# Gathering expert rows two experts ahead in a routed two-layer MLP behind attention

## The chip, the cores and the metric

One core of a Trainium2 chip runs the whole program in one launch. The metric is the device time of that launch in microseconds (us), the median over several runs. TensorE is PE in the profile (PEld is its weight load), VectorE DVE, ScalarE ACT, GpSimd POOL and SyncE SP.

## What is computed

Attention with normalised queries and keys (8 batches, 12 heads, 448 tokens, head size 64) gives 3584 token rows of 768 values. A hash of each token's id then picks one of 8 experts, and the row goes through that expert's two layers:

```python
expert_idx = token_ids * np.int64(2654435761) % np.int64(E)
for e in range(E):
    mask = expert_idx == e
    h = np.maximum(x[mask] @ w1[e], 0.0)    # w1[e]: 768 x 1024
    out[mask] = h @ w2[e]                   # w2[e]: 1024 x 768
```

## The kernel before, in words

The first stage, attention, writes its rows as 16-bit values to a scratch tensor in device memory (`x_scratch`), batch by batch, and builds a table `gidx` with the row numbers of each expert: four tiles of 128 rows (KT = 4, CAP = 512) for each of the 8 experts. A tile's first three quarters hold rows of the first seven batches only, so three of an expert's four tiles can be fetched before the last batch is stored; the fourth tile needs all batches.

The second stage, the experts, is what the change touches. For each expert `e` the loop at line 840 does this:

- `fetch` (lines 781 to 785) gathers tiles of 128 rows x 768 values (197 KB) from `x_scratch` into row buffers `xg`, one indirect DMA each, issued by POOL (line 173). The pool `m_xg` has 8 such buffers, zeroed once on DVE at lines 830 to 832.
- `gemm1` (line 747) multiplies w1 by the transposed rows `xT`: 48 matmuls, with ACT and DVE writing the result through a maximum with zero into `h_sb`.
- For each of the four tiles, `turn` (line 787) transposes one gathered tile of the *next* expert (six 128x128 transposes on PE at line 184 into the only buffer of `ps_x`, one DVE copy at line 185), and `gemm2` (line 761) makes one output tile of this expert: 16 matmuls (line 765), a copy to one of five `o_sb` buffers (line 769, ACT and DVE in turn), and an indirect DMA that scatters the 128 rows of 768 32-bit values (393 KB) to the output (line 770, POOL).
- `w_next` (line 813) issues weight pieces, also by POOL (line 816). An expert's weights come in six pieces that are converted from 32 to 16 bit on the way: four of 393 KB (w1) and two of 786 KB (w2). During expert `e` the six pieces of expert `e + 3` go out: two behind the gathers at its start, and one behind each of its four scatters. Two weight buffers each in `w_pool` and `w_pool2` hold four experts.

So POOL issues everything that moves in this stage, in program order: gathers, weight pieces, scatters. In the kernel before, expert `e + 1` is gathered at the start of expert `e` (line 848) and turned between the outputs of expert `e`.

Expert 0 differs. Its first three tiles are fetched and turned inside attention. Ahead of the loop (lines 833 to 838) the order is: three tiles of expert 1, one piece of expert 2's weights, the last tile of expert 0, the last tile of expert 1, the other five pieces of expert 2. In the loop, expert 0 first does `gemm1` for its first 384 rows and three outputs with no turns between them; then (lines 853 to 857) it turns its own last tile and all four tiles of expert 1 in a row, does `gemm1` for its last 128 rows, and the fourth output.

Of the kernel before, what the change touches and what calls it, by code (L numbers as in the profile page):

```python
# [19 lines left out]
def kernel(  # L20
# [16 lines left out]
    E = moe_w1.shape[0]  # L37
# [12 lines left out]
    KT = CAP // P  # L50
# [121 lines left out]
    def gather(xg, idx, rows=N):  # L172
        nc.gpsimd.indirect_dma_start(  # L173
            out=xg[:], out_offset=None, in_=x_dram[0:rows, :],
            in_offset=bass.IndirectOffsetOnAxis(ap=idx, axis=0),
            bounds_check=rows - 1, oob_is_err=False)
        return xg
# [3 lines left out]
    def put_xT(xg, xT, col, bank, copy=None):  # L181
        xT_ps = bank.rearrange("p (c t) -> p c t", c=CO)
        for co in range(CO):
            nc.tensor.transpose(xT_ps[:, co, :], xg[:, co * P:(co + 1) * P], ident16[:])  # L184
        (copy or nc.vector.tensor_copy)(xT[:, :, col * P:(col + 1) * P], xT_ps)  # L185
# [13 lines left out]
    with tc.manual_schedule(), \  # L199
# [461 lines left out]
        for g in range(1, NG):  # L661
            t = s0[g - 1]
# [69 lines left out]

    with tc.manual_schedule(), \
         tc.tile_pool(name="w_pool2", bufs=2) as w_pool2, \
         tc.tile_pool(name="m_xg", bufs=8) as m_xg, \
         tc.tile_pool(name="m_rt", bufs=1) as m_rt, \
         tc.tile_pool(name="m_x", bufs=2) as m_x, \
         tc.tile_pool(name="m_h", bufs=2) as m_h, \
# [8 lines left out]
        def gemm1(w1_sb, xT, h_sb, c0, c1):  # L747
            w1v = w1_sb[:].rearrange("p c (f o) -> p c o f", o=FO)
            for fo in range(FO):
                h_ps = ps_h.tile([P, 512], FP32, name="h_ps")  # L750
                for co in range(CO):
                    nc.tensor.matmul(h_ps[:, :c1 - c0], lhsT=w1v[:, co, fo, :],  # L752
                                     rhs=xT[:, co, c0:c1],
                                     start=(co == 0), stop=(co == CO - 1))
                if fo % 2 == 0:
                    nc.scalar.activation(h_sb[:, fo, c0:c1], h_ps[:, :c1 - c0], AF.Relu)  # L756
                else:
                    nc.vector.tensor_scalar(out=h_sb[:, fo, c0:c1], in0=h_ps[:, :c1 - c0],  # L758
                                            scalar1=0.0, scalar2=None, op0=ALU.max)

        def gemm2(w2_sb, h_sb, col, idx, free=True):
            o_ps = ps_o.tile([P, DIN], FP32, name="o_ps")
            for d0, d1 in ((0, 512), (512, DIN)):
                for fo in range(FO):
                    nc.tensor.matmul(o_ps[:, d0:d1], lhsT=h_sb[:, fo, col * P:(col + 1) * P],  # L765
                                     rhs=w2_sb[:, fo, d0:d1],
                                     start=(fo == 0), stop=(fo == FO - 1))
            o_sb = m_o.tile([P, DIN], FP32, name="o_sb")
            (nc.vector.tensor_copy if col % 2 else nc.scalar.copy)(o_sb[:], o_ps[:])  # L769
            scat = nc.gpsimd.indirect_dma_start(  # L770
                out=out[:, :], out_offset=bass.IndirectOffsetOnAxis(ap=idx, axis=0),
                in_=o_sb[:], in_offset=None, bounds_check=N - 1, oob_is_err=False)
            if free:

                tc.declare_no_dep(scat.ins, group="scatters", reason="disjoint rows")
                tc.add_to_no_dep_group("scatters", scat.ins)
# [4 lines left out]
        def fetch(e, kts):  # L781
            for kt in kts:
                c = e * KT + kt
                xgs[c] = gather(m_xg.tile([P, DIN], FP16, name="xg"), gidx[:, c:c + 1],
                                N_EARLY if kt < KT - 1 else N)

        def turn(e, kt):
            if e not in xTs:
                xTs[e] = m_x.tile([P, CO, CAP], FP16, name="xT")
            bank = ps_x.tile([P, DIN], FP16, name="xT_ps")  # L790
            put_xT(xgs.pop(e * KT + kt), xTs[e], kt, bank[:])

        def w_pieces(e):

            pool = wp(e)
            w1_sb = pool.tile([P, CO, F], FP16, name="w1_sb")
            w2_sb = pool.tile([P, FO, DIN], FP16, name="w2_sb")
            w_tiles[e] = (w1_sb, w2_sb)
            src1 = moe_w1[e].rearrange("(j ph hh pl) f -> ph pl hh j f", ph=2, hh=2, pl=64)
            src2 = moe_w2[e].rearrange("(p fo) d -> p fo d", fo=FO)  # L800
            dst1 = [w1_sb[64 * ph:64 * ph + 64].rearrange("p (hh j) f -> p hh j f", hh=2)
                    for ph in range(2)]
            res = []
            for ph in range(2):
                for hh in range(2):
                    res.append((dst1[ph][:, hh], src1[ph][:, hh]))
            for q4 in range(0, FO, 4):
                res.append((w2_sb[:, q4:q4 + 4], src2[:, q4:q4 + 4]))
            return res
# [3 lines left out]
        def w_next(n):  # L813
            for _ in range(min(n, len(queue))):
                o, i = queue.pop(0)
                nc.gpsimd.dma_start(out=o, in_=i)
# [5 lines left out]
        def overflow_table():  # L822
            nc.vector.tensor_tensor(out=ovc[:],
                                    in0=iota_f[:, 0:NOV, None].to_broadcast([P, NOV, E]),
                                    in1=oend[:, None, :].to_broadcast([P, NOV, E]), op=ALU.is_ge)
            nc.vector.reduce_sum(ovf[:], ovc[:], axis=AX.X)
            nc.vector.tensor_scalar(out=ov_i[:], in0=ovf[:], scalar1=float(E - 1), scalar2=None,
                                    op0=ALU.min)

        for t in range(8):  # L830
            z = m_xg.tile([P, DIN], FP16, name="xg")
            nc.vector.memset(z[:], 0.0)
        fetch(1, range(KT - 1))
# [1 line left out]
        w_next(1)  # L835
        fetch(0, [KT - 1])
        fetch(1, [KT - 1])
        w_next(len(queue))
        queue += w_pieces(3)
        for e in range(E):  # L840
            w1_sb, w2_sb = w_tiles[e]
            h_sb = m_h.tile([P, FO, CAP], FP16, name="h_sb")
            if e == 0:
                gemm1(w1_sb, xTs[e], h_sb, 0, EARLY)
                overflow_table()
            else:
                if e + 1 < E:
                    fetch(e + 1, range(KT))
                gemm1(w1_sb, xTs.pop(e), h_sb, 0, CAP)
            w_next(2)  # L850
            for kt in range(KT):
                c = e * KT + kt
                if e == 0 and kt == KT - 1:
                    turn(0, kt)
                    for k in range(KT):
                        turn(1, k)
                    gemm1(w1_sb, xTs.pop(0), h_sb, EARLY, CAP)
                elif e > 0 and e + 1 < E:
                    turn(e + 1, kt)
                gemm2(w2_sb, h_sb, kt, gidx[:, c:c + 1])  # L860
                w_next(1)
            w_next(len(queue))
            if e + 4 < E:
                queue += w_pieces(e + 4)
# [47 lines left out]
```

## Time and profile before

| | us |
|---|---|
| median of 3 timed runs (lowest to highest) | 421.67 (420.98 to 424.35) |
| the profiled execution's own time | 423.57 |
| its span, first to last instruction | 422.0 |
| PE busy in the span | 359.6 (85%) |
| DVE, ACT, POOL busy | 215.5, 187.4, 174.7 |

The profile's times are positions in the span, from its first instruction. The 1.57 us between the span and the execution's own time lie outside what the profile shows. Attention ends at about 191 us of the span, and the experts fill the rest. Numbers such as `x48` are counts of instructions; what stands in brackets behind a row of the timeline is the idle time of that engine ahead of it and what ended it.

### The profile page before, as it was taken

How to read it: one execution, taken by the hardware profiler on the slowest of the kernel's cores; microseconds unless marked ns; L12 is line 12 of the kernel's file. 1: busy time of each engine (PE TensorE's matmuls, PEld its weight loads, DVE VectorE, ACT ScalarE, POOL GpSimd, SP SyncE). 2: the span in 40 equal slices, each digit the busy share in tenths (PEclk: the TensorE clock that was granted, in tenths of full speed). 3: DMA queues.
4: the chain of work that ended last, by engine and by line, in shares of the span. 5: the costliest groups of instructions: out<-in, count | busy, mean ns of one | idle time of the engine just before them, and what ended most of it. 6: DMA issues, size and time to landing. Idle time of an engine off the chain costs nothing. (4 is left out here: it accounts for less than half of the span.)

```text
span 422.0 us, 9529 instructions
## 1 busy us (share of the span) xinstructions
PE 359.6 (85%) x4006; PEld 244.4 (58%) x4006; DVE 215.5 (51%) x517; ACT 187.4 (44%) x299; POOL 174.7 (41%) x247
## 2 busy tenths in 40 slices
PE   7776989899999999989898697895995987999970
PEld 3454767667676677657575364563563653666640
DVE  5665989989999999863232122221221321322210
ACT  3754989989999998961111011011110120121110
POOL 9897360046299200152716065262371450423030
PEclk9988999999999999989979699898898996999995
DMA  9999999829999960263999989899599691322020
GB/s 125 165 128 194 182 220 186 146 61 179 188 228 232 232 146 4 67 149 81 187 215 264 182 162 237 138 196 235 103 212 190 142 242 49 127 71 106 20 117 18
DMA packets 54268, 64.60 MB, mean 153 GB/s; under 512 B 22403, under 2 KB 42134, under 8 KB 53968
## 3 DMA queue, kind: packets, MB, share of 16 engines
q0 software_dynamic: 50592, 57.98, 79.0%
q1 hardware_dynamic: 3024, 5.41, 4.7%
q8 instruction: 32, 0.52, 0.5%
q10 hardware_dynamic: 608, 0.59, 0.5%
q14 instruction: 12, 0.10, 0.1%
HBM read 89.68 MB, written 18.09 MB: 255 GB/s over the span
## 5 line engine op out<-in xcount | busy, mean ns | idle before, releaser
L498 ACT ACTIVATE expT<-sc_ps 128x896 bf16<-128x896 f32 x144 | 123.9, 934 | 21.4 <-PE sc_ps L496 21.1
L765 PE MATMUL o_ps<-w_sb,h_sb 128*128 128x256 f16 (+1 forms) x512 | 96.8, 348 | 0.0
L770 POOL DMA_INDIRECT out_dram<-o_sb,gidx x32 | 33.0, 1032 | 118.1 <-ACT o_sb L769 82.9
L765 PEld LDWEIGHTS <-h_sb 128*128 128x128 f16 x512 | 52.0, 104 | 39.1 <-issue 10.0
L752 PEld LDWEIGHTS <-w_sb 128*128 128x128 f16 x432 | 59.8, 146 | 25.3 <-issue 0.8
L752 PE MATMUL h_ps<-xT,w_sb 128*128 128x512 f16 x336 | 73.7, 379 | 0.0
L769 ACT COPY o_sb<-o_ps 128x768 f32<-128x768 f32 x16 | 12.8, 799 | 102.7 <-PE o_ps L765 102.7
L756 ACT ACTIVATE h_sb<-h_ps 128x512 f16<-128x512 f32 (+2 forms) x36 | 19.7, 549 | 85.6 <-PE h_ps L752 85.6
L173 POOL DMA_INDIRECT xg<-x_scratch,gidx x32 | 32.6, 1019 | 59.1 <-DVE x_sb L536 38.3
L758 DVE TENSOR_SCALAR h_sb<-h_ps 128x512 f16<-128x512 f32 (+2 forms) x36 | 22.8, 632 | 59.5 <-PE h_ps L752 59.5
L520 PEld LDWEIGHTS <-expT 128*128 128x128 bf16 x1152 | 43.2, 98 | 9.8 <-issue 5.6
L496 PE MATMUL sc_ps<-qT,kT 64*128 64x448 f16 x288 | 43.5, 358 | 4.4 <-DVE et L385 1.4
L185 DVE COPY xT<-xT_ps 128x768 f16<-128x768 f16 x28 | 15.5, 555 | 61.2 <-PE xT_ps L184 61.2
L520 PE MATMUL av_ps<-v,expT 128*128 128x65 bf16 x1152 | 44.7, 195 | 0.0
L184 PE MATMUL xT_ps<-ident,xg 128*128 128x128 f16 x174 | 16.7, 241 | 26.4 <-DMA xg<-x_scratch,gidx 23.8
L769 DVE COPY o_sb<-o_ps 128x768 f32<-128x768 f32 x16 | 15.3, 958 | 39.8 <-PE o_ps L765 35.5
L475 PE MATMUL qkT_ps<-ident,n 128*128 128x128 f16 x384 | 30.6, 222 | 5.7 <-DVE n L320 3.6
L475 PEld LDWEIGHTS <-n 128*128 128x128 f16 x384 | 22.3, 98 | 20.0 <-issue 12.2
L184 PEld LDWEIGHTS <-xg 128*128 128x128 f16 x192 | 14.6, 108 | 32.0 <-DMA xg<-x_scratch,gidx 26.1
L536 DVE TENSOR_TENSOR x_sb<-av_ps,srec 128x448 f16<-128x448 f32 x48 | 29.7, 619 | 1.5
L287 PEld LDWEIGHTS <-ident 128*128 128x128 f16 x544 | 24.3, 99 | 7.7 <-issue 5.7
L503 ACT ACTIVATE expT<-sc_ps 128x448 bf16<-128x448 f32 x48 | 27.8, 578 | 1.6 <-PE sc_ps L501 1.6
(140 smaller groups left out, 403.2 us busy)
## 6 DMA issues: line engine op xcount, KB each, us to landing
w_sb<-in_moe_w_dram POOLq DMA_DIRECT2D x32, 384.0 KB, 12.0
w_sb<-in_moe_w_dram POOLq DMA_DIRECT2D x12, 768.0 KB, 11.6
x_scratch<-x_sb SPq DMA_DIRECT2D x15, 288.0 KB, 6.0
w_sb<-in_moe_w_dram POOLq DMA_DIRECT2D x2, 1536.0 KB, 16.8
kr<-in_k_dram POOLq DMA_DIRECT2D x6, 384.0 KB, 10.6
qr<-in_q_dram POOLq DMA_DIRECT2D x3, 768.0 KB, 14.8
vr<-in_v_dram POOLq DMA_DIRECT2D x6, 384.0 KB, 19.0
kr<-in_k_dram POOLq DMA_DIRECT2D x6, 288.0 KB, 9.6
```

The costliest lines, as they stand in the source:

```text
L173: nc.gpsimd.indirect_dma_start(out=xg[:], out_offset=None, in_=x_dram[0:rows, :], in_offset=bass.IndirectOffsetOnAxis(ap=idx, axis=0), bou ...
L184: nc.tensor.transpose(xT_ps[:, co, :], xg[:, co * P:(co + 1) * P], ident16[:])
L475: nc.tensor.transpose(T[:, o:o + P], n8[:, a, i, j].rearrange("p h d -> p (h d)"), ident16[:])
L496: nc.tensor.matmul(sc[:, hh, :S], lhsT=kT[64 * hh:64 * hh + 64, P * j:P * j + P], rhs=qT[64 * hh:64 * hh + 64, :], start=True, stop=True)
L498: nc.scalar.activation(expT[:, 2 * j:2 * j + 2, :], sc[:, :, :S], AF.Exp, bias=0.0, scale=1.0)
L503: nc.scalar.activation(expT[:, 6, :], sc[:, 0, :S], AF.Exp, bias=0.0, scale=1.0)
L520: nc.tensor.matmul(av[:, 2 * t + hh, :], lhsT=expT[:, tl(hh, j), P * t:P * t + P], rhs=v8[:, i, 4 * hh + j, 0:D + 1], start=(j == 0), stop ...
L536: nc.vector.tensor_tensor(out=x_sb[:, :, hp * D:hp * D + D], in0=av[:, :, :D], in1=srec[:, :, None].to_broadcast([P, SL, D]), op=ALU.mult)
L752: nc.tensor.matmul(h_ps[:, :c1 - c0], lhsT=w1v[:, co, fo, :], rhs=xT[:, co, c0:c1], start=(co == 0), stop=(co == CO - 1))
L765: nc.tensor.matmul(o_ps[:, d0:d1], lhsT=h_sb[:, fo, col * P:(col + 1) * P], rhs=w2_sb[:, fo, d0:d1], start=(fo == 0), stop=(fo == FO - 1))
L769: (nc.vector.tensor_copy if col % 2 else nc.scalar.copy)(o_sb[:], o_ps[:])
L770: scat = nc.gpsimd.indirect_dma_start(out=out[:, :], out_offset=bass.IndirectOffsetOnAxis(ap=idx, axis=0), in_=o_sb[:], in_offset=None, bo ...
```

## The change

Three edits. The row buffers become ten, and ten are zeroed. Expert `e + 2` is gathered at the start of expert `e` instead of expert `e + 1`, and to start with, all four tiles of expert 2 are gathered ahead of the loop, behind the last tile of expert 1 and in front of the five pieces of expert 2's weights. And expert 1's tiles are turned one ahead of each output of expert 0, as for the other experts, the last of them behind the second `gemm1` of expert 0.

```diff
-         tc.tile_pool(name="m_xg", bufs=8) as m_xg, \
+         tc.tile_pool(name="m_xg", bufs=10) as m_xg, \
...
-        for t in range(8):
+        for t in range(10):
             z = m_xg.tile([P, DIN], FP16, name="xg")
             nc.vector.memset(z[:], 0.0)
         fetch(1, range(KT - 1))
...
         w_next(1)
         fetch(0, [KT - 1])
         fetch(1, [KT - 1])
+        fetch(2, range(KT))
         w_next(len(queue))
...
             else:
-                if e + 1 < E:
-                    fetch(e + 1, range(KT))
+                if e + 2 < E:
+                    fetch(e + 2, range(KT))
                 gemm1(w1_sb, xTs.pop(e), h_sb, 0, CAP)
             w_next(2)
             for kt in range(KT):
                 c = e * KT + kt
                 if e == 0 and kt == KT - 1:
                     turn(0, kt)
-                    for k in range(KT):
-                        turn(1, k)
                     gemm1(w1_sb, xTs.pop(0), h_sb, EARLY, CAP)
-                elif e > 0 and e + 1 < E:
+                    turn(1, kt)
+                elif e + 1 < E:
                     turn(e + 1, kt)
                 gemm2(w2_sb, h_sb, kt, gidx[:, c:c + 1])
                 w_next(1)
```

## Rows read from the trace of the kernel before

**Rows 1.** The page's 40 equal slices of the span: granted clock and DMA share, in tenths.
```profile
PEclk9988999999999999989979699898898996999995
DMA  9999999829999960263999989899599691322020
```

**Rows 2.** Waits of PE from 185 us on: us in total, times, longest.
```profile
PE xT_ps L184 <- DMA xg<-x_scratch,gidx: 23.8, 5, 6.0
```

**Rows 3.** Windows, one per expert 1 to 6: busy and count by engine, clock, DMA share, GB/s.
```profile
219.67:250.12 30.45, 24.44 (x139) 15.20 (x138) 6.82 (x10) 3.98 (x6) 12.14 (x14) 0.89 0.96 215
250.12:278.13 28.01, 23.73 (x138) 14.94 (x137) 6.82 (x10) 3.98 (x6) 12.14 (x15) 0.94 0.92 186
278.13:307.80 29.67, 24.76 (x139) 15.37 (x138) 6.82 (x10) 3.98 (x6) 12.16 (x15) 0.88 0.84 176
307.80:335.99 28.19, 23.90 (x139) 15.02 (x137) 6.82 (x10) 3.98 (x6) 12.17 (x15) 0.94 0.90 184
335.99:365.45 29.46, 25.10 (x138) 15.56 (x137) 6.82 (x10) 3.99 (x6) 8.69 (x10) 0.88 0.53 138
365.45:387.55 22.10, 22.10 (x138) 14.46 (x137) 6.73 (x10) 3.99 (x6) 8.05 (x8) 1.00 0.28 95
```

**Rows 4.** Timeline of PE, first tile of gemm2 for experts 1 and 6.
```profile
236.21 0.82 PE L184 MATMUL xT_ps<-ident,xg 128*128 128x128 f16 x6 [6.01 <-DMA xg<-x_scratch,gidx]
236.82 4.65 PE L765 MATMUL o_ps<-w_sb,h_sb 128*128 128x512 f16 x16
241.31 0.50 PE L184 MATMUL xT_ps<-ident,xg 128*128 128x128 f16 x6
...
375.81 0.50 PE L184 MATMUL xT_ps<-ident,xg 128*128 128x128 f16 x6
...
378.75 0.50 PE L184 MATMUL xT_ps<-ident,xg 128*128 128x128 f16 x6
```

**Rows 5.** Timeline of PE, late attention and expert 0.
```profile
177.70 0.62 PE L475 MATMUL qkT_ps<-ident,n 128*128 128x128 f16 x8
...
195.00 4.06 PE L752 MATMUL h_ps<-xT_e,w_sb 128*128 128x384 f16 x24 [0.65 <-DVE h_sb L758]
198.90 7.96 PE L765 MATMUL o_ps<-w_sb,h_sb 128*128 128x512 f16 x48
206.70 0.50 PE L184 MATMUL xT_ps<-ident,xg 128*128 128x128 f16 x6
207.85 0.49 PE L184 MATMUL xT_ps<-ident,xg 128*128 128x128 f16 x6 [0.65 <-DVE xT_e L185]
...
210.14 0.80 PE L184 MATMUL xT_ps<-ident,xg 128*128 128x128 f16 x6 [0.65 <-DVE xT L185]
...
212.18 5.06 PE L752 MATMUL h_ps<-xT_e,w_sb 128*128 128x128 f16 x48
```

**Rows 6.** Timeline of POOL, ahead of and in the first two experts.
```profile
197.78 1.05 POOL L173 DMA_INDIRECT xg<-x_scratch,gidx  x1 [11.36 <-DVE h_sb L758]
...
200.14 4.31 POOL L816 DMA_DIRECT2D w_sb<-in_moe_w_dram  x7
204.75 1.08 POOL L770 DMA_INDIRECT out_dram<-o_sb,gidx  x1 [0.30 <-issue]
...
231.44 0.65 POOL L816 DMA_DIRECT2D w_sb<-in_moe_w_dram  x1 [2.39 <-DMA w_sb<-in_moe_w_dram]
```

**Rows 7.** Windows: the long queue of experts 0 and 1, and the gap behind it.
```profile
204.00:234.00 30.00, 23.60 (x161) 17.24 (x158) 8.64 (x15) 4.29 (x9) 12.56 (x15) 0.88 1.07 232
...
242.00:244.00 2.00, 2.00 (x14) 1.16 (x12) 0.40 (x1) 0.31 (x1) 1.40 (x2) 1.00 0.03 4
```

**Rows 8.** DMA issues at 197.7 to 198.5 us, then 222 to 228: count, us to landing.
```profile
xg<-x_scratch,gidx POOLq DMA_INDIRECT x1, 3.0
...
xg<-x_scratch,gidx POOLq DMA_INDIRECT x4, 12.9
```

**Rows 9.** Timeline of DVE, the last of the eight buffer clears.
```profile
183.58 0.38 DVE L832 MEMSET xg<- 128x384 uint32 x1
```

## The prediction

> **What bounds the kernel now.** I read the 40 slices of the page first, then the waits of PE, then windows cut at the start of each expert's `gemm1`, then the timelines of PE and POOL inside one expert. In the slices the clock dips again and again in the second half of the span, where the experts run, while DMA stays near full until about 350 us and is little used from there on [rows 1]. The waits say why PE stops there: 23.8 us in five waits of a transpose for gathered rows [rows 2]. That is one wait for each of the experts 1 to 5. Expert 6 has the same work with its rows there in time, and takes 22.10 us at full clock, PE busy throughout; experts 1 to 5 take 30.45, 28.01, 29.67, 28.19 and 29.46 [rows 3]. The reader should see in the PE timeline what such a wait costs twice over: at expert 1 it lasts 6.01 us, and the first transposes and output behind it take 241.31 - 236.21 = 5.10 us where expert 6 needs 378.75 - 375.81 = 2.93 [rows 4]. The clock granted in these experts averages 0.88 to 0.94 against 1.00 [rows 3]: after the idle stretch PE runs for a while at 1.2 GHz and not 2.4. So the stage is bound by PE plus a wait for rows on each expert, and the wait comes from order, not from a slow gather: alone a gather lands 3.0 us after issue, behind weight pieces 12.9 us [rows 8].
>
> **Experts 1 to 5.** With rows gathered one expert earlier, a tile is issued some 22.1 + 10.5 us before its turn, where now it has only the `gemm1` of one expert. If the rows come in time each expert takes expert 6's 22.10. The sum of the five steps is 145.8, less 5 x 22.1 = 110.5: **-35.3 us** [rows 3]. Of it 23.8 is the wait itself [rows 2], the rest clock. Nothing is added to PE or DVE in these steps: the same turns stand at the same places. On POOL the same four gathers stand at the same place, only for another expert; from expert 6 on none are left.
>
> **Expert 0.** Now three outputs without turns take 206.70 - 198.90 = 7.80, or 2.60 each; then come five turns 1.15 apart (206.70 to 207.85), each waiting 0.65 for DVE to empty the one transpose buffer; the fourth turn already runs at half rate (0.80 for what took 0.50), and so does the small `gemm1` behind them, 48 matmuls in 5.06 [rows 5]. `gemm1` of expert 1 starts at 219.67 [rows 3], 20.77 after 198.90. Afterwards: three outputs with a turn each, 3 x 2.93 = 8.8 (expert 1's first three tiles were gathered inside attention and wait already); one turn and its gap, 1.15; the small `gemm1`; a turn, 0.34; an output, 2.60. One gap of 0.65 did not cost the clock at 195.00, where 24 matmuls of 384 columns took 4.06 [rows 5], so I expect the small `gemm1` at 2.4 GHz. Its bounds are 4.9 (as now) and half of that, 2.45; eight transposes of as many columns took 0.62 [rows 5], 78 ns each at most, or 3.7 for 48, last one's drain included each time. I take 2.9, nearer the half. Sum 15.8, so expert 1 starts at 214.7: **-5.0 us** (bounds -5.4 and -3.0).
>
> **Two more clears.** 2 x 0.38 on DVE [rows 9], in the last attention steps. Bounds 0 and +0.8; DVE has idle room behind 184 us, so **+0.2**.
>
> **The moved gathers on POOL.** Four gathers, about 1.3 each with their gap, stand ahead of seven weight pieces that now start at 200.14 and of the first scatter at 204.75 [rows 6]. Pieces and scatters of expert 0 go out some 5.2 late, and POOL has caught up by the fourth scatter (four pairs of scatter and piece, 1.8 each, against outputs 2.93 apart). Behind them wait expert 2's weights, which land by about 220 and are needed at 236.8, and five output buffers, of which expert 0 fills four. **0 us**. If that cover were gone it would cost the 5.2. A further buffer conflict I rule out by order: with ten buffers the four new rows go where rows of an expert already turned lay.
>
> **What is late next: DMA.** This is the only large unknown. Per expert that carries weights the queue moves 4 x 0.393 + 2 x 0.786 (weights) + 4 x 0.393 (scatters) + 4 x 0.197 (gathers) = 5.5 MB. With a long queue, 204 to 234 us, it wrote 232 GB/s [rows 7], which gives 23.7 us per expert. At expert 2 the step of 28.01 had a DMA share of 0.92 [rows 3], 25.8 us of work; the queue ran dry inside that step as it did at 242 us [rows 7], and started again one scatter at a time. Either is above PE's 22.1, so DMA falls behind by 1.6 to 3.7 us per expert, against a cushion. The cushion: expert 2's first tile landed at 236.21 [rows 4] through a queue that stayed full from 202; the same queue with four more gathers (0.79 MB, 3.4 us) lands expert 3's at 239.6, and they are needed at 214.7 + 22.1 + 10.5 = 247.3. That leaves 7.7 us, and four more experts (gathers for 4 to 7) eat at it. With DMA time d per expert, the stall at the end is 4 x (d - 22.1) - 7.7: none at 23.7, 1.9 at 24.5, 7.1 at 25.8. In the new order the queue is always long, so I stand nearer the first row: d = 24.4, **+1.5 us**, at experts 5 and 6. Output buffers have nearly the same cushion (the third scatter of an expert lands about half of d behind the gathers ahead of it and is needed 11.7 us behind them), so they wait with the gathers and not on top. Weights have more: expert 7's are through just ahead of its gathers, about 337 to 343, and needed at 347. POOL already waits at times for an earlier transfer before it issues (2.39 at 231.44 [rows 6]); it will do that more, which moves no landing while the queue is full.
>
> The Trainium skill ("HBM Reference", Specifications) gives a core about 358 GB/s as its share of device memory, and about 425 streaming alone. Counted at that memory a weight byte written is two bytes read, so an expert costs 6.3 + 1.6 + 0.8 = 8.7 MB, an estimate of 24.2 us at the share and 20.4 alone: the page's first figure makes DMA the later one and adds 0.7 us to the time, its second leaves PE the later. At an expert's mix (8.7 to 5.5) the 232 GB/s written [rows 7] are 367 at the memory, and that stretch held more weights than the mix, so this trace already passes the share, if not by much.
>
> **Sum.** 423.57 - 35.3 - 5.0 + 0.2 + 1.5 = 385.0 for an execution like the profiled one. That one was 1.9 above the median of the timed runs, so I forecast **383 us** for the median, -9%.
>
> **The rivals.**
> 1. *DMA takes over.* The weight stream sets the pace and waits for rows come back, shorter, at experts 4 to 6. For it: the share near 1 [rows 3]; against: gaps as at 242 [rows 7]. With d = 25.8 it is 7.1 in place of 1.5 and perhaps two dips of the clock at 2.2 each (5.10 - 2.93 [rows 4]): 393. If d were the 28.0 of a whole present step, 4 x 5.9 - 7.7 = 15.9: 397.
> 2. *The clock stays low in expert 0.* The small `gemm1` takes 4.9 and a gap or two more dip: 385 to 388. For it: it fell at 210.14 after a few gaps of 0.65 [rows 5]; against: only one of these gaps is left.
> 3. *Slower: PE at 1.2 GHz through expert after expert.* If DMA throttles every output by a short wait, PE could alternate between work and gap as at 207 to 210, where the clock fell [rows 5]. An expert at the low level takes twice 22.1 at worst, +22 us; the gain of 40 is gone, and 4 more with it, once two experts' worth run so. At d = 25.8 the wait is only 3.7 per expert, in one or two places, so this needs much more than rival 1.
> 4. *It does not do what it says.* The wait is put down to the gather that came last; if scatters or weights were due at the same moment, PE would wait for them instead, and the time stays within 1%. Against: in the gap at 242 the queue had run empty [rows 7], so all else had landed too.
>
> **How the numbers follow.** Chances: forecast (stall 0 to 4) 0.67, rival 1 0.16, rival 2 0.10, rival 4 0.04, rival 3 0.03. About 1%, 4 us, is what a measurement of this kernel can tell from no change. Forecast and rivals 1 and 2 are all faster by more: 0.93; rival 4 is the same: 0.04; rival 3 slower: 0.03. Low end: no stall, a gain of 5.4 in expert 0: 381, less 1.5 for the spread of runs, 379.5. The high end takes in rival 2 and the first case of rival 1: 393.
>
> **What would show it.** Right: no wait of PE for `xg` in experts 1 to 4, steps of 22.1 to 23 at clock 1.00, `gemm1` of expert 1 near 214.7, weights through by about 340. Gathers land later than now (10 to 20 us) and nobody waits. Wrong: waits for `xg` or for `o_sb` at experts 2 to 4 already, or steps that settle at 24 to 26 (rival 1); a small `gemm1` near 5 us (rival 2); steps above 30 at a clock of 0.5 to 0.7 (rival 3); the same five waits with another releaser (rival 4).

## The result, and the profile after

The changed kernel takes 385.29 us (median of 4 runs, 380.92 to 387.3) against 423.01 for the kernel before (4 runs): a ratio of 0.9088, 95% interval 0.8964 to 0.9213. Ratios and their intervals, here and below, leave out executions in a slower state, here the highest of each four. The changed kernel's profiled execution took 386.59 us, its span 385.0. The forecast was 383, its range 379.5 to 393.

The DMA share in the slices of the page, as in [rows 1], now stays full to about 340 us:

```profile
DMA  8999999943999999103548999999999999932030
```

Four of the waits from 185 us on (us in total, times, longest): POOL's to issue a weight piece, which was 5.2 us in five; those of ACT and DVE for a scatter to free an output buffer, which the kernel before did not have; and PE's for rows, which was 23.8 in five [rows 2]:

```profile
POOL w_sb L816 <- DMA w_sb<-in_moe_w_dram: 28.2, 15, 3.6
ACT o_sb L769 <- DMA out_dram<-o_sb,gidx: 24.7, 4, 6.7
...
DVE o_sb L769 <- DMA out_dram<-o_sb,gidx: 20.3, 6, 3.8
...
PE xT_ps L184 <- DMA xg<-x_scratch,gidx: 2.3, 2, 1.2
```

The windows of experts 1 to 6, with the columns of [rows 3]: what took 30.45, 28.01, 29.67, 28.19 and 29.46 takes 22.10, 22.10, 22.88, 23.76 and 23.90, and the granted clock is 1.00 in all of them.

```profile
213.81:235.91 22.10, 22.10 (x138) 14.47 (x137) 6.73 (x10) 3.99 (x6) 9.41 (x11) 1.00 1.07 239
235.91:258.01 22.10, 22.10 (x138) 14.46 (x137) 6.73 (x10) 3.99 (x6) 10.99 (x13) 1.00 1.10 234
258.01:280.89 22.88, 22.44 (x139) 14.37 (x137) 6.75 (x10) 3.99 (x6) 11.60 (x14) 1.00 1.06 208
280.89:304.65 23.76, 22.43 (x139) 14.41 (x137) 6.82 (x10) 3.99 (x6) 12.12 (x14) 1.00 1.07 220
304.65:328.55 23.90, 22.44 (x139) 14.39 (x138) 6.82 (x10) 3.99 (x6) 12.16 (x15) 1.00 1.05 216
328.55:350.65 22.10, 22.10 (x139) 14.47 (x138) 6.73 (x10) 3.99 (x6) 7.98 (x9) 1.00 0.56 186
```

The timeline of PE in expert 0, against [rows 5]: a turn ahead of each output, one gap of 0.65, the small `gemm1` from 207.90 to the next turn at 210.88, and `gemm1` of expert 1 at 213.81.

```profile
197.95 0.50 PE L184 MATMUL xT_ps<-ident,xg 128*128 128x128 f16 x6
...
207.90 3.14 PE L752 MATMUL h_ps<-xT_e,w_sb 128*128 128x128 f16 x48 [0.65 <-DVE xT_e L185]
210.88 0.50 PE L184 MATMUL xT_ps<-ident,xg 128*128 128x128 f16 x6
```

Gathers now take longer to land than before, and PE loses little by it. DMA issues from 300 to 306 us (count, us to landing), against 12.9 [rows 8]:

```profile
xg<-x_scratch,gidx POOLq DMA_INDIRECT x4, 15.5
```

These are expert 6's rows, and PE waits 1.11 us for the first of them at 316.28. They go out late: POOL has fallen behind PE. Its timeline shows the start of the long queue, the fourth scatter of expert 0, and the first gather of expert 5's rows, which the program issues at the start of expert 3 (258.01):

```profile
204.42 4.32 POOL L816 DMA_DIRECT2D w_sb<-in_moe_w_dram  x7
...
225.15 1.02 POOL L770 DMA_INDIRECT out_dram<-o_sb,gidx  x1 [1.69 <-DVE h_sb L758]
...
276.63 1.06 POOL L173 DMA_INDIRECT xg<-x_scratch,gidx  x1 [0.37 <-DMA out_dram<-o_sb,gidx]
```

The first two stops of PE behind expert 1's start are these:

```profile
277.96 0.49 PE L184 MATMUL xT_ps<-ident,xg 128*128 128x128 f16 x6 [0.33 <-DVE xT L185]
...
292.65 0.51 PE L184 MATMUL xT_ps<-ident,xg 128*128 128x128 f16 x6 [1.24 <-DMA xg<-x_scratch,gidx]
```

The second is for expert 5's rows, which thus went out 14.8 us ahead of their turn. The first is not for rows: DVE emptied the transpose buffer late, because its output copy just ahead (276.48) had stood 3.79 us for a scatter to free an output buffer.

In the two profiled executions the 37.0 us between 423.57 and 386.59 are: 0.95 because expert 0's outputs start at 197.95 and not 198.90; 4.91 in expert 0 (20.77 to 15.86); 31.04 in experts 1 to 6 (167.88 to 136.84, the sums of the windows); 0.1 behind.

### The profile page after: what moved, and what is told of

It is laid out like the page before. It is cut to its first block, busy times and chain, and to the rows that moved or that the text cites. A ratio compares the mean times of both kernels' runs of the same rounds, so it can differ in the third digit from the quotient of the medians.

```text
span 385.0 us, 9539 instructions
## 1 busy us (share of the span) xinstructions
PE 344.5 (89%) x4006; PEld 236.8 (62%) x4006; DVE 216.0 (56%) x519; ACT 187.5 (49%) x299; POOL 175.1 (45%) x247
## 5 line engine op out<-in xcount | busy, mean ns | idle before, releaser
L765 PE MATMUL o_ps<-w_sb,h_sb 128*128 128x256 f16 (+1 forms) x512 | 87.9, 326 | 0.0
L752 PEld LDWEIGHTS <-w_sb 128*128 128x128 f16 x432 | 58.0, 144 | 25.7 <-issue 1.6
L765 PEld LDWEIGHTS <-h_sb 128*128 128x128 f16 x512 | 48.9, 98 | 32.6
L816 POOL DMA_DIRECT2D w_sb<-in_moe_w_dram x36 | 23.1, 645 | 30.2 <-DMA w_sb<-in_moe_w_dram 28.2
L185 DVE COPY xT<-xT_ps 128x768 f16<-128x768 f16 x28 | 15.5, 554 | 23.9 <-PE xT_ps L184 23.8
L485 DVE TENSOR_SCALAR kT<-qkT_ps,g_col 128x512 f16<-128x512 f16 x48 | 23.1, 481 | 9.5 <-PE qkT_ps L475 8.4
```

## The experiments

My theory (A) behind the prediction: rows wait because they stand behind weights, and once they are early enough PE sets the pace, with DMA's time per expert eating at a cushion. Rivals: the two edits simply add up; the five output buffers are what is late next. The "excess" below is what the windows of experts 1 to 6 take above 6 x 22.10 us, worked out as above (4.24 for the profiled execution). Ratios are against runs of the kernel before on the same chip.

**One edit at a time.** Two-ahead gathers with expert 1's turns in a row as before:

```diff
                 if e == 0 and kt == KT - 1:
                     turn(0, kt)
+                    for k in range(KT):
+                        turn(1, k)
                     gemm1(w1_sb, xTs.pop(0), h_sb, EARLY, CAP)
-                    turn(1, kt)
-                elif e + 1 < E:
+                elif e > 0 and e + 1 < E:
```

> The changed kernel, but with expert 1's four tiles turned in a row behind expert 0's third output, as before the change. Theory A (DMA time against a cushion): expert 0 takes about 20.8 us from its first output to gemm1 of expert 1 instead of 15.9, but the queue gains the same 5 us on PE, so most of the 4.2 us by which experts 3 to 5 exceed 22.1 us in the changed kernel goes away; the time is 0 to 2 us above the changed kernel. Rival (the two edits add up): 5 us above it, and experts 3 to 5 still exceed 22.1 us by about 4.

Measured: 386.09 us, ratio 0.9139 (0.9052 to 0.9226). Expert 0 takes 19.43 us (198.63 to 218.06), and the excess is zero; experts 1 to 6 all stand at 22.10, the fifth in this window:

```profile
306.46:328.56 22.10, 22.10 (x138) 14.48 (x137) 6.72 (x10) 3.98 (x6) 11.91 (x14) 1.00 1.05 219
```

The opposite kernel is the kernel before with only the turns moved (eight row buffers, rows one expert ahead).

> The kernel before with only expert 1's turns put between expert 0's outputs; rows are gathered one expert ahead from eight buffers. Theory A: expert 0 is 5 us shorter, but expert 2's rows still land at about 236 us because the queue is full from 202 us, so PE's wait for them at expert 1 grows from 6.0 to about 10 or 11 us and the time is within 1 us of before. Rival (the edits add up): 5 us below before, waits unchanged.

Measured: 425.22 us, ratio 1.0014 (0.9944 to 1.0084): no change. Its PE timeline at expert 1 shows why. Expert 1 starts at 213.03 instead of 219.67, and the rows of expert 2 land at 236.27 where they landed at 236.21 [rows 4]; the wait grows from 6.01 to 12.72.

```profile
213.03 10.52 PE L752 MATMUL h_ps<-xT,w_sb 128*128 128x512 f16 x48
236.27 0.82 PE L184 MATMUL xT_ps<-ident,xg 128*128 128x128 f16 x6 [12.72 <-DMA xg<-x_scratch,gidx]
```

The edits don't add up: the turns alone bring nothing, where 5 us would be a ratio of 0.988, outside the interval; the gathers alone bring nearly all. What the turns add behind the gathers these intervals leave open. Ten buffers without the earlier gathers were not run; in the kernel before no gather from 223 us on stands more than 0.64 us ahead of its issue, so none was waiting for a buffer.

**What the last waits come from.** Eight output buffers (`m_o`, `bufs=8`):

> The changed kernel with eight output buffers instead of five. Theory A (DMA throughput sets the rest): the waits of DVE and ACT for a scatter to free an output buffer vanish, but rows come no earlier, so PE's waits for rows grow by about what the others lose, and experts 3 to 5 still exceed 22.1 us by 3 to 4.5 in sum. Rival (five output buffers are what is late): the excess falls to 2.3 or less.

Three pieces of expert 2's weights instead of one ahead of the last tiles (`w_next(3)` for `w_next(1)`):

> The changed kernel with three pieces of expert 2's weights issued ahead of the last tiles of experts 0 and 1 instead of one, in a stretch where the queue is empty. Theory A: 0.79 MB, about 3.4 us of DMA work, moves into idle time, the cushion grows by it, and experts 3 to 5 exceed 22.1 us by 0 to 1.5 in sum: 3 to 4 us below the changed kernel. Rival (each step is paced by its own transfers or by output buffers): the excess stays at 3.5 to 4.5. Against it in both: the last tile of expert 0 could land too late for its turn near 206.8 us, and PE would wait there.

Measured: 384.29 us (ratio 0.9107, 0.9028 to 0.9187) with an excess of 0.97, and 384.37 (0.9123, 0.9042 to 0.9205) with an excess of zero. By its own bound the first spoke for the rival, and I first read it so. With eight buffers one wait of PE for rows was left, 0.8 us at expert 6.

Expert 2's rows behind the pieces instead of in front:

```diff
-        fetch(2, range(KT))
         w_next(len(queue))
+        fetch(2, range(KT))
```

> The changed kernel with expert 2's four tiles gathered behind the five weight pieces instead of in front. Theory A: the rows have time to spare (needed near 224 us, landed by 217 to 220), nobody waits for them, the weight pieces start some 5 us earlier and DMA gains 1 to 2 us on PE; the excess of experts 3 to 5 falls from 4.2 to between 2 and 3.5. Rival (the place in front of the pieces matters): PE waits for rows at expert 1 by 2 us or more.

Measured: an excess of zero in its one execution, in which attention ended some 6 us later. The next three runs put it beside the changed kernel, and with eight output buffers as well:

> The changed kernel once more, on the chip of the next two runs, for comparison: ratio to before 0.90 to 0.92, excess of experts 3 to 5 over 22.1 us between 3 and 5 in sum, clear of how fast attention happened to run.

> Expert 2's rows behind the weight pieces, timed. Theory A: an excess of 0 again, so 3 to 4 us (about 1% of the time before) below the changed kernel on the same chip. Rival (the excess of 0 of the first look was chance, from attention that ran 5 us slower there): excess 3 to 5, the same time.

> Both: expert 2's rows behind the pieces and eight output buffers. Theory A: nothing is left to remove in experts 1 to 6, which all stand at PE's 22.10, so no gain over the former run beyond 0.5 us. Rival (the queue still costs PE something elsewhere): 1 us or more below it.

Measured: 384.28 us for the changed kernel (ratio 0.9035, 0.8986 to 0.9083), 383.19 (0.9003, 0.8951 to 0.9056) and 383.31 (0.9012, 0.8962 to 0.9062). None is told apart from the changed kernel. And the changed kernel's own excess was 0.49 this time, not 3 to 5, while the one with the rows behind had 1.51 instead of its former zero. The excess varies from one execution to the next by as much as these edits were to move it, so the single executions above settle nothing about buffers or order; my reading of them falls. In the changed kernel's two executions the rate of the queue differs as well. The windows from 204 to 330 us, first of its first profile (excess 4.24), then of its second (0.49); the last column is GB/s written:

```profile
204.00:330.00 126.00, 122.12 (x785) 80.14 (x783) 37.80 (x59) 21.85 (x35) 63.67 (x76) 1.00 1.06 220
```

```profile
204.00:330.00 126.00, 125.02 (x799) 82.85 (x797) 38.91 (x61) 23.04 (x37) 64.84 (x77) 1.00 1.06 228
```

5.5 MB at these rates are 25.0 and 24.1 us per expert; over four experts that is 3.5 us, and the two excesses differ by 3.75. This fits A, but it does not show the cause: a stall of 3.75 us in 126 is 3.0%, the rates differ by 3.5%, and the first execution with the rows behind wrote 223 in this window without any excess.

What does sort the six executions with five output buffers and all the weights is how long ACT and DVE wait for a scatter to free a buffer: 45.0 us in the first profile of the changed kernel (excess 4.24), 21.7 in the timed one with the rows behind (1.51), 14.0 in the second of the changed kernel (0.49), and none in the three with an excess of zero. With eight buffers these waits are gone, and the excesses are 0.97 and zero. A scatter that frees its buffer late also stands in the queue and behind POOL, so this does not tell buffers and queue apart.

**Less and more to move.** These edits change more than that. First the changed kernel without the w2 pieces of experts 4 to 7; it computes their outputs with the w2 of experts 0 to 3.

```diff
-            w2_sb = pool.tile([P, FO, DIN], FP16, name="w2_sb")
+            w2_sb = (pool.tile([P, FO, DIN], FP16, name="w2_sb") if e < 4
+                     else w_tiles[e - 4][1])
...
-            for q4 in range(0, FO, 4):
+            for q4 in range(0, FO if e < 4 else 0, 4):
```

> The changed kernel without the two w2 pieces of experts 4 to 7 (their outputs are made with the w2 of experts 0 to 3): 1.57 of 5.5 MB less per expert. Theory A (what is left of the wait comes from DMA time per expert above PE's 22.1 us): DMA time falls from about 24.4 to 17.4 us, experts 1 to 6 all take 22.10 and no wait for rows or for a scatter is left. Rival (five output buffers are too few whatever the queue carries): experts 3 to 5 still exceed 22.1 us by 2 or more in sum.

Measured: an excess of 0.12, no wait for rows, with five output buffers. Attention ended 4.7 us later in this execution, so its one time (386.86) says nothing of that. The window of expert 4 shows the queue no longer full:

```profile
285.14:307.24 22.10, 22.10 (x139) 14.48 (x138) 6.73 (x10) 3.98 (x6) 10.98 (x12) 1.00 0.80 173
```

Then a w1 piece of experts 4 to 7 loaded a second time, with eight and with five output buffers:

```diff
+            if e >= 4:
+                res.append((dst1[1][:, 1], src1[1][:, 1]))
```

> The changed kernel with eight output buffers, and one w1 piece of experts 4 to 7 loaded a second time: 0.393 MB more per expert in the steps of experts 1 to 4, at about 225 GB/s 1.75 us each. Theory A: the excess over 22.1 us per expert rises from the 1.0 measured with eight output buffers by 4 x 1.75 to about 8 (6 to 9), in the last experts, as waits for rows. Rival (the queue has room and the piece hides): below 2.

> The same extra piece with the five output buffers of the changed kernel. Theory A: the excess rises from 4.2 by about 7 to some 11 (9 to 13), waits for an output buffer first among them. Rival: below 5.5.

Measured: excesses of 26.1 (steps of 22.10, 22.10, 31.73, 23.12, 31.80 and 27.86) and 18.6, far more than either theory gave. The edit did more than I meant: the second load writes where the first does, and POOL now stood up to 8.6 us for an earlier weight piece to land, with everything behind it. POOL's timeline:

```profile
263.00 0.65 POOL L818 DMA_DIRECT2D w_sb<-in_moe_w_dram  x1 [8.44 <-DMA w_sb<-in_moe_w_dram]
```

In the window from 242.48 to 264.58 the DMA share fell to 0.85. So the extra piece got a tile of its own, which nobody reads, with eight output buffers:

```diff
+            if e >= 4:
+                spare = m_sp.tile([P, CO // 2, F], FP16, name="spare")
+                res.append((spare[64:P], src1[1][:, 1]))
```

> Eight output buffers, and 0.393 MB more per expert for experts 4 to 7, this time into a tile of its own that nobody reads, so that no transfer has to wait for another. Theory A: at 225 GB/s 1.75 us more per expert over four experts, so the excess rises from 1.0 to about 8 (6 to 10), in the later experts, as waits of PE for rows, without POOL standing 8 us at one weight piece as in the two former runs. Rival (any extra piece breaks the order of the queue): an excess near 26 again.

Measured: an excess of 13.2. POOL's longest wait at a weight piece is 3.7 us here. The waits of PE for rows are 8.1 us, the size that A gave, and come from the third expert on. The other 5 I had left out: at two of the waits the clock fell to 1.2 GHz (0.82 for what takes 0.50), as in the kernel before. Waits of PE, then the window and the PE timeline of expert 4, where both are seen:

```profile
PE xT_ps L184 <- DMA xg<-x_scratch,gidx: 8.1, 4, 3.8
```

```profile
281.25:310.14 28.89, 25.05 (x138) 15.48 (x137) 6.82 (x10) 3.99 (x6) 14.10 (x18) 0.88 1.07 219
```

```profile
295.62 0.82 PE L184 MATMUL xT_ps<-ident,xg 128*128 128x128 f16 x6 [3.84 <-DMA xg<-x_scratch,gidx]
```

So more to move brings the waits for rows back: 7% more cost 13 us in this one execution, three times the largest excess of the changed kernel; for output buffers ACT and DVE wait 5.6 us in two waits, and PE's waits are for rows. That 29% less removes them is not shown, since other executions come to zero with the full load.

## Why the prediction was right, and where it was off

- *What bounds the kernel.* Right: with rows early, experts 1 and 2 take exactly the 22.10 us of expert 6 at full clock. Gathers that take 15.5 us to land cost PE 2.3 us in all where 12.9 cost 23.8, so it was order and not the gather.
- *Expert 0.* 15.86 us against 15.8; the small `gemm1` took 2.98 against 2.9. The clock held through one gap, so rival 2 did not happen. But "-5.0" is no term of its own, which the prediction did not say: by itself the edit brings nothing (1.0014), since a shorter expert 0 only waits longer for rows. What it adds on top of the gathers is not measured to better than a few us (ratio 0.9139 without it, 0.9035 to 0.9088 with it, the intervals overlap).
- *Experts 1 to 5.* The term of -35.3 holds but for what is late next, which was mis-sized: +1.5 at experts 5 and 6 was forecast, 4.24 came in the first profile, at experts 3 to 5, and 0.49 in the second. The step that was off is the cushion. Expert 3's first tile was to land at 239.6 and be needed at 247.3, 7.7 us later; in the first profile it was issued at 227.84 and landed 16.2 us behind that, at 244.0, and was needed at 246.3: a cushion of 2.2. Expert 7's landed at 338.4, so four experts took 23.6 us each, below my 24.4. The prediction's own formula gives 4 x (23.6 - 22.1) - 2.2 = 3.8 with these, beside 4.24. In the second execution the cushion is 4.4, the time per expert 23.25, and the formula gives 0.2, beside 0.49. This is an account after the fact, since a stall of PE also holds back scatters. As far as it goes the mechanism held, and two sizes were off in opposite directions. Output buffers did not "wait with the gathers and not on top": in the first profile PE's first loss, at expert 3, came through them, with no wait for rows yet.
- *The rule weighed.* The Trainium skill ("HBM Reference", Specifications) gave, by a core's share of about 358 GB/s, an estimate of 24.2 us per expert. With the queue full, this case gives 24.1 and 25.0 by the rates and 23.6 and 23.25 by the landings, so I was too quick to put the share aside on one stretch of 30 us that held a different mix. But that page of the Trainium skill gives the share for two cores that stream at once, and about 425 GB/s for a core alone, as in this program. By the second figure the estimate was 20.4 us, and no run here reached it; what holds this mix below it is not shown.
- *The moved gathers on POOL.* The "0 us" was too small. With four gathers ahead of them the seven weight pieces start at 204.42 and not at 200.14, so the queue that was to be full from 202 fills 4.3 us later. That is as much as expert 3's rows were late in the first profile (244.0 for 239.6); in the second they landed at 241.5 in the same order, so it need not be the whole cause. Nor had POOL caught up by the fourth scatter of expert 0: it went out at 225.15, 11 us behind the end of its output (213.97). The five output buffers covered for that only up to expert 3. And rows gathered one expert earlier were not issued 22.1 + 10.5 us ahead of their turn: 14.8 at expert 5's.
- *Two more clears.* No loss seen: the outputs of expert 0 start 0.95 us earlier, where a third turn in attention kept the clock (0.49 us, 0.80 before). Attention itself starts and ends some us apart between executions, so I claim nothing for it.
- *The sum.* For an execution like the profiled one 385.0 was forecast, and 386.59 came. The last waits were 2.7 us above their term, and 1.15 us of that is hidden because expert 0 began 0.95 us earlier where 0.2 later was put down. That the total came this near is partly luck, as is a second execution in which hardly any wait was left.
- *Rival 1* came in a mild form: the share is 1.05 to 1.10 through experts 1 to 5 and a few us come back. Its full form needs a little more load, as the last experiment shows. *Rival 4* fell with the 22.10 of experts 1 and 2, and *rival 3* with a clock of 1.00.

## What to carry to other kernels

When an engine waits for a transfer that is fast alone, look for what stands ahead of it in the queue, and move its issue by a whole stage rather than making it faster. Two edits that shorten the same path must not be summed before asking which of them is behind the other's wait: here the gathers alone are worth nearly 9%, and the turns alone nothing. And once an engine and the queue take nearly equal times per stage, the difference accumulates from stage to stage, so give the cushion and the number of stages with the forecast, and check the cushion against everything that starts the queue later: here it was the term that was off.

## What I had not expected

An extra 0.393 MB that had to wait for an earlier transfer into the same place cost 26.1 us of excess; the same bytes into a tile of their own cost 13.2, with the same eight output buffers. Each is one execution. In program order the scatters and gathers stand behind a piece that waits (8.44 us at 263.00). And one kernel's queue wrote 220 GB/s in one execution and 228 in another, with last waits of 4.24 and 0.49 us; which of the two brings the other, and why they differ, stays open.
